# Threshold attention and a maxout layer on one core: the order of the work written out as one list in place of steps

## The chip, the core and the metric

The kernel runs on one core of a Trainium2 chip. Its engines work side by side, each through its own instructions in order: TensorE (PE, with the weight loads as PEld), VectorE (DVE), ScalarE (ACT), GpSimd (POOL), and SyncE (SP), which here only issues DMAs. The metric is the time of one execution on the device in microseconds (us), less is better.

## The reference

Eight batches of eight heads, 576 rows and 64 columns a head. For each head:

```python
scores = scale * q @ k.T                         # 576 x 576
thresh = max(scores, row) - tau                  # tau = 0.02
scores = where(scores >= thresh, scores, -1e9)
attn   = softmax(scores)
x      = attn @ v                                # heads side by side: x is 4608 x 512
```

Then the maxout layer over all 4608 rows, with weights 512 x 768 and 768 x 512:

```python
h   = maximum(maximum(x @ w1, x @ w2), x @ w3)
out = h @ w_out
```

## The kernel before

**Attention.** A quad is four heads of one batch; there are 16 (`quads`), two a batch. `load` and `load_v` (L153, L177) bring a quad in, with ten DMAs on SP. Four pieces a quad (`transposed`, L228: q and k, two pairs of heads each) turn q and k on PE; ScalarE writes the scaled q (`qt`), VectorE writes k (`kt`), GpSimd writes `qs`, a copy of `qt` with the halves of the partitions exchanged (`swapped`, L215). `cast_v` (L193) makes v bf16 on GpSimd. A *chunk* is one block of 128 rows of queries for two of the heads (indices 0 to 8 in a quad, 144 in all). It has two *tiles*, r = 0 and 1, each 128 x 576 scores in float32. For each tile:

- `scores` (L253): matmuls on PE into a PSUM slot, the two halves of the contraction rows at once.
- `maximum` (L280): VectorE finds the row maximum in that slot.
- `exponents` (L291): ScalarE reads the slot and writes `z`. With this the slot is free.
- `numerators` (L299): a tile is *masked* or not (`masked`, L277). If it is, ScalarE has already taken exp, and VectorE zeroes what lies under the threshold and sums (SCALAR_TENSOR_TENSOR). If it isn't, ScalarE has written Prelu with a very flat side, and a second ScalarE pass takes exp and sums.

Then, for the chunk, `normalized` (L308): a reciprocal on VectorE, two products to bf16 on GpSimd (`P`), and a DMA transpose from SP into `pt` ("ptq"). When the nine chunks of a quad are there, `product` (L317) multiplies by v on PE, once for each r, and copies to `xt`, on VectorE or ScalarE or both.

**Maxout layer.** When both quads of a batch are done, `ffn` (L377) yields 18 hidden pieces (6 blocks of 128 columns times w1, w2, w3) and three output pieces. A hidden piece of a whole batch has two halves of eight matmuls, the second behind a wait for the first (`halves`, L355), since both write the same banks. The w1 result goes through ScalarE to `hm`, the others are joined to it by VectorE (`hm`, `hT`). Output pieces go through ScalarE (`ob`, `obr`) and SP to memory. The last batch is done in two parts of 256 and 320 rows.

**PSUM and buffers.** All PSUM is one pool of four slots of 128 x 1024 float32, given out round robin (`slot`, L149). `z` has four buffers, `P` six.

**What sets the order.** `_Ordered` (L53) keeps each of the four compute engines in the order in which the program issues. That order comes from steps, one a chunk (`step`, L573). `others(n)` (L515) chooses what joins step n: what `plan` has for its two half steps (the four transpose pieces of the next quad at half steps 9, 11, 13, 15, the products at PA = 12 and PB = 14 of the quad after), or else a piece each from `todo`, the list of maxout pieces. PE gets these and the scores of chunk n + 1, in an order like this; a and b are halves of pieces, s are scores:

```python
ARRAY = "a0 a1 b0 b1 s0 s1"
ORDER = "V0 A0 R0 K0 V1 M0 M1 A1 N0 K1 N1 E0 E1"
LAG = dict(M=0, E=0, N=1, K=1)
```

ORDER is the same in every step: V and A are the copies out of PSUM on VectorE and ScalarE, M maxima, E exponents, N and K numerators (not masked, masked) of the chunk before, R the normalization. Loads come at the start of a quad's steps (L610 to L613), value casts at step 1 for the first quad and step 3 of each quad for the next, the twelve loads of the weights at steps 12, 14, ... 34 with their casts two steps later. `masked` is the same for all quads: the r = 1 tile of six of the nine chunks, of seven in the first three quads, 99 tiles of 288.

Of the kernel before, what the change touches and what calls it, by code (L numbers as in the profile page):

```python
# [23 lines left out]
EARLY = 3  # L24
MASKED0 = (0, 1, 2, 3, 4, 6, 7)
MASKED = (0, 1, 3, 4, 6, 7)
# [3 lines left out]
ARRAY = "a0 a1 b0 b1 s0 s1"  # L30
ORDER = "V0 A0 R0 K0 V1 M0 M1 A1 N0 K1 N1 E0 E1"
LAG = dict(M=0, E=0, N=1, K=1)
LATE = 0
ED = 40
HOLD = 0
WL = (12, 14, 16, 18, 20, 22, 24, 26, 28, 30, 32, 34)
WC = 2
LQ = 0
LV = 0
NC = 3  # L40
TS = (9, 11, 13, 15)
PA = 12
PB = 14


class _Piece:


    def __init__(self, first, second=None, done=None, on=""):
        self.first, self.second, self.done, self.on, self.needs = first, second, done, on, None  # L50
# [23 lines left out]
def kernel(  # L74
# [23 lines left out]
    tensor, scalar, vector, pool = (_Ordered(tc, e) for e in (nc.tensor, nc.scalar, nc.vector, nc.gpsimd))  # L98
# [18 lines left out]
    def weight_loads():  # L117


        def piece(dst, src):  # L120
            my = {}

            def load():
                my["t"] = stage.tile([128, 4 * 256], F32, name="stage")
                nc.sync.dma_start(out=my["t"].rearrange("p (k f) -> p k f", k=src.shape[1]), in_=src)

            def cast():
                pool.tensor_copy(out=dst, in_=my["t"].rearrange("p (k f) -> p k f", k=src.shape[1]))
            return load, cast
# [11 lines left out]
    zz = ctx.enter_context(tc.tile_pool(name="zz", bufs=4))  # L141
    pp = ctx.enter_context(tc.tile_pool(name="pp", bufs=6))
# [4 lines left out]
    ps_s = ctx.enter_context(tc.tile_pool(name="ps_s", bufs=4, space=PSUM))  # L147

    def slot(name):  # L149
        return ps_s.tile([128, 1024], F32, name=name, tag="s")  # L150


    def load(g, first=False):  # L153
        b, qd = quads[g]
        L = dict(b=b, qd=qd, first=first)
        q2 = nc.scalar if first else nc.sync
# [7 lines left out]
        srcs = (("q", q, nc.sync), ("k", k, q2))  # L164
# [12 lines left out]
    def load_v(g, L):  # L177
# [4 lines left out]
        for h in range(4):  # L182
            nc.sync.dma_start(out=vm[:, h].rearrange("p c d -> p (c d)"),
                              in_=v[b, 4 * qd + h].rearrange("(p c) d -> p (c d)", c=9)[:, 0:512]
                              .rearrange("p (x u) -> p x u", x=2))
        for r in range(2):
            nc.sync.dma_start(out=vr[64 * r:64 * r + 64], in_=src[:, 8, 2 * r:2 * r + 2, :])
# [40 lines left out]
    def transposed(L, n, r):  # L228
# [5 lines left out]
        def first():  # L234
            targets(L, n)
            st["ps"] = ps = slot("tp")
# [7 lines left out]
        def done():  # L244
            off = 320 * r
            evacuated(L, n, r, lambda t: t[:, :, off:off + 64 * nj],
                      st["ps"].rearrange("p (i z) -> p i z", i=2)[:, :, 0:64 * nj])
            if n == "q":
                swapped(L, slice(off, off + 64 * nj))
        return _Piece(first, None, done, "A" if n == "q" else "V")  # L250


    def scores(L, idx, r):  # L253

        ps = slot("sc")
# [21 lines left out]
    def masked(g, idx, r):  # L277
        return r == 1 and idx in (MASKED0 if g < EARLY else MASKED)

# [28 lines left out]
    def normalized(L, idx, z, sm):  # L308
        rs = small.tile([128, 2], F32, name="rs")
        vector.reciprocal(rs, sm)  # L310
        P = pp.tile([128, W], BF16, name="P")
        for n in range(2):
            pool.tensor_scalar(out=P[:, n * S:(n + 1) * S], in0=z[:, n * S:(n + 1) * S],
                                    scalar1=rs[:, n:n + 1], scalar2=1.0, op0=OP.mult, op1=OP.mult)
        nc.sync.dma_start_transpose(out=L["pt"][:, :, idx * 128:(idx + 1) * 128], in_=P)

    def product(L, r, xt, part=None):  # L317
# [11 lines left out]
        def first():  # L329
            st["ps"] = ps = slot("o")  # L330
# [7 lines left out]
        def done():  # L338
            ps = st["ps"]
            dst = xt[:, 2 * L["qd"] + r, :]  # L340
            if part is None and r == 0:
                vector.tensor_copy(out=dst, in_=ps[:, 0:S])
            elif part is None:
                vector.tensor_copy(out=dst[:, 512:S], in_=ps[:, 512:S])
                scalar.activation(out=dst[:, 0:512], in_=ps[:, 0:512], func=AF.Copy)
            elif part == 1:
                scalar.activation(out=dst[:, 0:256], in_=ps[:, 0:256], func=AF.Copy)
            elif r == 0:
                vector.tensor_copy(out=dst[:, 256:S], in_=ps[:, 0:320])
            else:  # L350
                scalar.activation(out=dst[:, 256:S], in_=ps[:, 0:320], func=AF.Copy)
        return _Piece(first, None, done, "A" if part == 1 or part == 2 and r == 1 else "V")
# [24 lines left out]
    def ffn(b, xt, hT, runs, chunks):  # L377


        st = {}  # L380
        nr, n = len(runs), runs[0][1] - runs[0][0]

        def hid(f, wi):
            my = {}

            def start():
                if wi == 0:
                    st["hm"] = hp_.tile([128, nr, n], BF16, name="hm", bufs=3)
                my["hm"], my["ps"] = st["hm"], slot("ph")

            def operands(kc, a):
# [3 lines left out]
                        lambda rows: xt[rows, kc, c0:c1])  # L395

            def first():
                start()
# [8 lines left out]
            def done():  # L407
                hm = my["hm"]
# [3 lines left out]
                else:  # L412
                    dst = hm if wi == 1 else \
                        hT[:, f, runs[0][0]:runs[-1][1]].rearrange("p (a u) -> p a u", a=nr)
                    vector.tensor_tensor(out=dst, in0=pv, in1=hm, op=OP.max)
            return [_Piece(first, (lambda: my["h"][1]()) if nr == 2 else None, done, "V" if wi else "A")]
# [3 lines left out]
        def outp(c):  # L420
# [3 lines left out]
            def first():  # L424
                my["ps"] = ps = slot("po")
                my["h"] = halves([[(ps[:, 512 * a:512 * a + 512],
                                    lambda rows, a=a, f=f: hT[rows, f, (c + a) * 128:(c + a) * 128 + 128],
# [3 lines left out]
            def done():  # L431
                for a in range(2):
                    ob = hp_.tile([128, DM], F32, name="ob", bufs=4)
                    scalar.activation(out=ob, in_=my["ps"][:, 512 * a:512 * a + 512], func=AF.Copy)
                    nc.sync.dma_start(out=rows_out[:, (0, 2, 1, 3)[c + a]:8:4], in_=ob)
            return [_Piece(first), _Piece(lambda: my["h"][1](), None, done, "A")]

        def ninth():
# [3 lines left out]
            def first():  # L442
                my["ps"] = ps = slot("po")
                for f in range(NF):
                    for x in range(2):
                        tensor.matmul(ps[64 * x:64 * x + 64, :256], hT[:, f, 512:S], wo[:, f, 256 * x:256 * x + 256],
                                      start=(f == 0), stop=(f == NF - 1))

            def done():
                ob = hp_.tile([128, DM // 2], F32, name="obr", bufs=2)  # L450
                scalar.activation(out=ob, in_=my["ps"][:, :256], func=AF.Copy)
                for x in range(2):
                    nc.sync.dma_start(out=rows_out[:, 8, 256 * x:256 * x + 256], in_=ob[64 * x:64 * x + 64])
            return [_Piece(first, None, done, "A")]

        return ([pc for f in range(NF) for wi in range(3) for pc in hid(f, wi)],
# [12 lines left out]
    Ls, xts, hTs = {}, {}, {}  # L469
    todo, held = [], []  # L470

    def o_step(g, r, part=None):
        b = quads[g][0]
        if b not in xts:
            xts[b] = xp.tile([128, 4, S], BF16, name="xt")
        mine = [product(Ls[g], r, xts[b], part)]
        if r == 1 and quads[g][1] == 1:
            if b not in hTs:
                hTs[b] = hp_.tile([128, NF, S], BF16, name="hT")
            if part is None:  # L480
                runs, chunks = ((0, S // 2), (S // 2, S)), (0, 2, 4)
            elif part == 1:
                runs, chunks = ((0, 256),), (0,)
            else:
                runs, chunks = ((256, S),), (2, 4)
            hids, outs = ffn(b, xts[b], hTs[b], runs, chunks)
            hids[0].needs = mine[0]
            for o in outs:
                o[0].needs = hids[-1]

            todo.extend(hids + held + [p for o in outs[:-1] for p in o])
            held[:] = outs[-1]
        return mine


    plan = {}

    def at(when, fn):
        plan.setdefault(when, []).append(fn)

    prep = [("q", 0), ("k", 0), ("q", 1), ("k", 1)]
    for g in range(NQ - 2):
        for when, a in zip(TS, prep):
            at(18 * g + when, lambda g=g, a=a: [transposed(Ls[g + 1], *a)])
        at(18 * g + 18 + PA, lambda g=g: o_step(g, 0))
        at(18 * g + 18 + PB, lambda g=g: o_step(g, 1))
    e = 18 * y
    for when, a in zip((0, 1, 4, 5), prep):
        at(e + when, lambda a=a: [transposed(Ls[z_], *a)])
    for when, g, pr in zip((15, 17, 23, 25), (y, y, z_, z_), (0, 1, 0, 1)):  # L510
        at(e + when, lambda g=g, pr=pr: o_step(g, pr, 1))
    for when, g, pr in zip((34, 35), (y, y), (0, 1)):
        at(e + when, lambda g=g, pr=pr: o_step(g, pr, 2))

    def others(n):  # L515

        ps = []
        for when in (2 * n, 2 * n + 1):
            if when in plan:
                for fn in plan[when]:  # L520
                    ps.extend(fn())
            else:
                for _ in range(2 if when >= e + ED else 1):
                    if todo and n >= HOLD:
                        ps.append(todo.pop(0))
        return ps

    def issued(ps, scored=()):

        scored = list(scored)
        out = []
        if len(ps) == 2 and ps[0].second and ps[1].needs is not ps[0]:
# [138 lines left out]
```

## Time and profile before

| | |
|---|---|
| three timed runs | 492.9, 493.21, 494.25 us (median 493.21) |
| profiled execution | span 493.0 us, first to last instruction |
| TensorE's mean granted clock | 0.965 |
| VectorE: row maxima | 288 of about 750 ns |
| VectorE: second pass of masked tiles | 99, mean 886 ns |
| ScalarE: exponents, second pass, its accumulator read | 288 of 741, 189 of 692, 189 of 210 ns |
| GpSimd: normalization | 288 of 768 ns, two a chunk |
| GpSimd: `qs` copies; value casts; weight casts | 62 of 835; 16 of 1134 and 32 of 290; 12 of about 1100 ns |
| DMA transposes | 144, each 1.3 us of SP's issue, landing after 3.8 us (3.2 to 7.6) |

Rows of the profile name an engine, an operation and "out<-in" by the names of the tiles: `sc` scores, `nm` and `unused` the maxima (masked or not), `z` exponents, `rs` reciprocals, `P` and `ptq` the normalized block and its transpose, `o` products with v, `tp` transposes, `ph` hidden, `po` outputs. A wait "A <- B" says that A sat idle until B ended. All compute lines carry L62, the helper in `_Ordered`, so rows are told apart by tiles.

### The profile page before, as it was taken

To read this page: it belongs to the slowest core of one execution; us is meant where nothing else is said; L and a number is where in the kernel's file an instruction comes from. 1 tells how busy PE (TensorE), PEld (TensorE's weight loads), DVE (VectorE), ACT (ScalarE), POOL (GpSimd) and SP (SyncE) were. 2 spreads that over 40 slices of the span, in tenths; PEclk is the share of its full clock that TensorE was granted. 3 is DMA by queue.
4 is the path that set the end of the run, shared out by engine and by line. 5 is a ranking of instruction groups with operands and counts; after the bars stand their busy time and mean duration, and the time that the engine had idled before them with its cause. 6 is when DMAs were issued, how large, how long until landed. Compare 5 with 4: busy or idle time off the path is not lost.

```text
span 493.0 us, 14020 instructions
## 1 busy us (share of the span) xinstructions
PE 457.5 (93%) x5188; PEld 309.4 (63%) x5188; DVE 401.2 (81%) x996; ACT 394.5 (80%) x814; POOL 308.4 (63%) x416
## 2 busy tenths in 40 slices
PE   7777879979999999999999999999999989999995
PEld 5434437747477675767577675867567665676672
DVE  3998977968799979899798978899799998788350
ACT  3998978857998889888998889889898897886322
POOL 3797989876675757475665857475665776444000
PEclk8797978979999999999999999999999999999999
DMA  7899999999999999969699879979696556854402
GB/s 222 278 195 224 183 263 206 252 237 229 187 210 192 191 196 207 213 138 202 141 231 169 175 158 203 217 132 201 148 238 145 99 96 147 143 100 93 126 12 97
DMA packets 213285, 87.44 MB, mean 177 GB/s; under 512 B 186336, under 2 KB 200160, under 8 KB 213216
## 3 DMA queue, kind: packets, MB, share of 16 engines
q1 hardware_dynamic: 212656, 85.95, 83.3%
q8 instruction: 41, 0.67, 0.6%
q10 hardware_dynamic: 560, 0.59, 0.4%
q14 instruction: 28, 0.23, 0.2%
HBM read 34.60 MB, written 9.44 MB: 89 GB/s over the span
## 4 chain that ended last, share of the span: by engine, by line
PE 54%; DVE 12%; POOL 11%; ACT 11%; issue 7%; DMA 5%; SPq 0%; ACTq 0%; POOLq 0%; DVEq 0%
PE ph L62 21%; PE sc L62 18%; PE po L62 8%; ACT z L62 8%; POOL P L62 7%; PE o L62 5%; DVE unused L62 5%; DMA ptq<-P 3%; DVE z L62 3%; POOL qs L62 2%; DVE nm L62 2%; PE tp L62 1%; ACT ob L62 1%; DVE hm L62 1%; DMA qm<-in_q_dram 1%
## 5 line engine op out<-in xcount | busy, mean ns | idle before, releaser
L62 POOL TENSOR_SCALAR P<-z,rs 128x576 bf16<-128x576 f32 x288 | 217.5, 768 | 121.7 <-DVE rs L62 95.7
L62 ACT ACTIVATE z<-sc,nm 128x576 f32<-128x576 f32 x288 | 198.1, 741 | 51.3 <-DVE unused L62 28.5
L62 PE MATMUL sc<-kt,qs 64*128 64x256 f32 (+2 forms) x640 | 193.4, 444 | 11.6 <-ACT z L62 9.8
L62 PE MATMUL sc<-kt,qt 64*128 64x320 f32 (+2 forms) x640 | 194.3, 456 | 7.3 <-ACT z L62 7.0
L62 DVE TENSOR_SCALAR_CACHE_REDUCE unused<-sc 128x576 bf16<-128x576 f32 x189 | 138.4, 749 | 30.9 <-PE sc L62 30.4
L62 PE MATMUL ph<-xt,w 64*128 64x288 bf16 (+2 forms) x2160 | 162.1, 283 | 1.2 <-ACT z L62 0.6
L62 PEld LDWEIGHTS <-w 64*128 64x128 bf16 (+1 forms) x2160 | 127.4, 94 | 31.8 <-issue 11.8
L62 ACT ACTIVATE z<-z 128x576 f32<-128x576 f32 x189 | 129.5, 692 | 0.0
L62 PEld LDWEIGHTS sc<-kt,qs 64*128 64x128 f32 (+1 forms) x640 | 92.3, 184 | 44.0 <-ACT z L62 34.0
L62 PEld LDWEIGHTS sc<-kt,qt 64*128 64x128 f32 (+1 forms) x640 | 92.8, 184 | 29.5 <-ACT z L62 27.0
L62 DVE SCALAR_TENSOR_TENSOR z<-z 128x576 f32<-128x576 f32 x99 | 87.7, 886 | 0.0
L62 DVE TENSOR_REDUCE nm<-sc 128x1 f32<-128x576 f32 x99 | 74.5, 752 | 1.1 <-PE sc L62 1.0
L62 POOL COPY qs<-qt 64x640 f32<-64x640 f32 (+1 forms) x62 | 51.8, 835 | 14.7 <-ACT qt L62 11.7
L62 DVE TENSOR_TENSOR hm<-ph,hm 128x576 bf16<-128x576 f32 (+2 forms) x54 | 37.3, 690 | 23.9 <-PE ph L62 14.3
L62 PE MATMUL po<-wo,hT 64*128 64x512 bf16 (+1 forms) x480 | 52.4, 357 | 0.4
L62 PE MATMUL o<-ptq,vb 128*64 128x64 bf16 (+2 forms) x544 | 42.3, 293 | 4.0 <-DMA ptq<-P 4.0
L62 PEld LDWEIGHTS <-hT 64*128 64x128 bf16 (+1 forms) x480 | 26.2, 97 | 23.8 <-issue 5.1
L62 ACT ACTIVATE hm<-ph 128x576 bf16<-128x576 f32 (+2 forms) x54 | 32.2, 597 | 11.1 <-PE ph L62 11.1
L62 PEld LDWEIGHTS <-vb 128*64 128x64 bf16 x544 | 23.1, 114 | 26.8 <-issue 14.8
L62 ACT ACTIVATION_READ_ACCUMULATOR z<-z 128x1 f32 x189 | 39.7, 210 | 0.0
L62 DVE TENSOR_TENSOR hT<-ph,hm 128x576 bf16<-128x576 f32 (+2 forms) x54 | 37.1, 687 | 2.5 <-PE ph L62 0.8
L62 ACT ACTIVATE qt<-tp 128x640 f32<-128x640 f32 (+1 forms) x32 | 21.1, 660 | 9.3 <-PE tp L62 9.3
(30 smaller groups left out, 246.7 us busy)
## 6 DMA issues: line engine op xcount, KB each, us to landing
vm<-in_v_dram SPq DMA_DIRECT2D x64, 128.0 KB, 2.9
out_dram<-ob SPq DMA_DIRECT2D x32, 256.0 KB, 2.6
qm<-in_q_dram SPq DMA_DIRECT2D x15, 512.0 KB, 4.5
km<-in_k_dram SPq DMA_DIRECT2D x15, 512.0 KB, 5.3
stage<-in_moe_w_dram SPq DMA_DIRECT2D x9, 512.0 KB, 4.7
ptq<-P SPq DMA_TRANSPOSE x144, 3.8
stage<-in_moe_w_out_dram SPq DMA_DIRECT2D x3, 512.0 KB, 4.5
qm<-in_q_dram SPq DMA_DIRECT2D x16, 64.0 KB, 3.3
```

Source lines behind the costliest of these rows:

```text
L62: ins = fn(*a, **kw)
```

## The change

The step machinery (`plan`, `others`, `issued`, `step`, `rest` and their constants) goes. In its place stands one string for 2445 pieces of work, read from left to right by `issue`. A letter is one piece of work, taken from the front of a line of work that is ready for that letter. S, T, O and F start scores, transposes, products and maxout pieces on PE and are followed by a digit, the PSUM slot. B is the second half of the oldest maxout piece that has one. Small letters are: m maxima, e exponents, n and k numerators, r reciprocal, p normalization, t the DMA transpose, a and c copies of transposed q and k, q the exchanged copy, h, v and u copies of maxout pieces, w and x copies of products, y value casts, l the loads of a quad, g and z the load and the cast of a piece of weights, o a store.

The four PSUM slots become four pools of one buffer, named by the digit. Which tiles are masked is a string of 288 digits with 106 ones, in either r. SP joins the engines that keep the order of issue. Buffers (`z` 4, `P` 6) and the work on each piece stay as they were.

```diff
-EARLY = 3
-MASKED0 = (0, 1, 2, 3, 4, 6, 7)
-MASKED = (0, 1, 3, 4, 6, 7)
+MASKED = """
+001001010001010101001000111000011001001101001100100100000100100010001000
...
-ARRAY = "a0 a1 b0 b1 s0 s1"
-ORDER = "V0 A0 R0 K0 V1 M0 M1 A1 N0 K1 N1 E0 E1"
...
+ORDER = """
+lS0myeS1nS2mS3emnS0mleS1rpemT2knS3meamT0erqcS2nT1kS0emapS3trmnS1emytemS2ekT0ecpS3lnmS1nS0rmpemnS2kqemeS3meS1
+rkepT0mntS2rampektS0nmT3erctpeS1mnT3S2tkyameS3tnrrmS0pemngS1mpetrkeS2mepS3tmeS0mnS1gqketrnmT2emlpekS3nkO0qem
+nrcS1eprwS2nS3rmnS0pmemeS1mpeO2tmnrkepS3tekS0nmS1ztxwrmepS2rnmtS3ekzetmS0npmS1etmerT2kpntS3marmepS2tkeT0mnS1
+tceermS3pgnT0kgS2emqtaS1rmnO0merepkS3ewS2nmpT1tO0nmecztekS3xzS1wrmngF2pmS0geBkeS3mqhtF1meBrreS2pvS0nmF3nF1mz
...
-    tensor, scalar, vector, pool = (_Ordered(tc, e) for e in (nc.tensor, nc.scalar, nc.vector, nc.gpsimd))
+    tensor, scalar, vector, pool, sync = (
+        _Ordered(tc, e) for e in (nc.tensor, nc.scalar, nc.vector, nc.gpsimd, nc.sync))
...
-    ps_s = ctx.enter_context(tc.tile_pool(name="ps_s", bufs=4, space=PSUM))
-
-    def slot(name):
-        return ps_s.tile([128, 1024], F32, name=name, tag="s")
+    ps_s = ctx.enter_context(tc.tile_pool(name="ps_s", bufs=1, space=PSUM))
+
+    def bank(name, where):
+        return ps_s.tile([128, 1024], F32, name=name, tag=f"s{where}")
...
     def masked(g, idx, r):
-        return r == 1 and idx in (MASKED0 if g < EARLY else MASKED)
+        return by_mask[2 * number[g, idx] + r] == "1"
...
-                    nc.sync.dma_start(out=rows_out[:, (0, 2, 1, 3)[c + a]:8:4], in_=ob)
...
+                stores.append(lambda: sync.dma_start(out=rows_out[:, (0, 2, 1, 3)[c + a]:8:4], in_=ob))
...
+    def issue(what, where):
+        if what == "S":
+            c, r = next(todo["S"])
+            c[r] = scores(Ls[c["g"]], c["idx"], r, where)
+            line["m"].append((c, r))
...
+        elif what == "m":
+            c, r = line["m"].pop(0)
+            c["bias", r] = maximum(c["g"], c["idx"], r, c[r])
+            line["e"].append((c, r))
...
+    while x < len(text):
+        what = text[x]
+        if what in "STOF":
+            x += 1
+        issue(what, int(text[x]) if what in "STOF" else None)
+        x += 1
```

## The prediction

> **What bounds the kernel now.** I read the busy rows and the slices first: an order can only win where the engine that bounds a stage stands still.
>
> ```profile
> PE 457.5 (93%) x5188; PEld 309.4 (63%) x5188; DVE 401.2 (81%) x996; ACT 394.5 (80%) x814; POOL 308.4 (63%) x416
> ...
> PE   7777879979999999999999999999999989999995
> ...
> PEclk8797978979999999999999999999999999999999
> ```
>
> PE is at seven or eight tenths in the first six slices and again in the ninth (98.6 to 111 us), then at nine. So there are stages with different limits. VectorE's timeline gives the borders by the first maximum of a chunk (a chunk is one block of 128 query rows of two heads, two score tiles): chunk 0 at 9.3 us, chunk 18 at 56.2, chunk 26 at 79.7, chunk 36 at 116.1, chunk 126 at 395.2, the last at 449.4. The table of stretches, cut there (length, busy us of PE, PEld, DVE, ACT, POOL, then granted clock, DMA share, GB/s):
>
> ```profile
> 9.30:56.20 46.90, 38.13 (x284) 22.12 (x284) 42.56 (x110) 40.68 (x84) 38.95 (x51) 0.83 0.95 225
> 56.20:79.70 23.50, 18.24 (x142) 10.71 (x141) 18.68 (x50) 18.40 (x39) 20.31 (x25) 0.78 1.11 245
> 79.70:116.10 36.40, 33.33 (x396) 24.17 (x395) 29.27 (x73) 27.77 (x58) 29.79 (x38) 0.91 1.06 232
> 116.10:395.20 279.10, 272.57 (x3296) 187.44 (x3290) 246.50 (x611) 244.05 (x505) 183.21 (x253) 1.00 0.92 183
> ```
>
> To 56.2, DVE (91%) and ACT (87%) set the pace, 2.44 us a chunk where nothing stands. From 56.2 to 79.7 POOL is the fullest (86%) and the DMA share is over 1. From 116.1 on PE is busy 97.7%, at 3.1 us a chunk. The chain of waits inside 95 to 112 us shows what an early stall is made of:
>
> ```profile
> 95.74 0.98 POOL vb L62
> 96.72 0.12 POOL vr L62
> 96.84 7.59 DMA ptq<-P
> 104.43 0.04 issue
> 104.48 2.61 PE o L62 x14
> ```
>
> POOL's value casts delay a softmax block, its transpose goes out late on a full queue, and PE, which runs in order, stands before the product that reads it. Last, the waits of 116.1 to 395.2 (total, times, longest):
>
> ```profile
> PEld sc L62 <- ACT z L62: 30.0, 89, 1.0
> DVE unused L62 <- PE sc L62: 22.5, 39, 2.3
> ...
> PE sc L62 <- ACT z L62: 4.8, 11, 0.5
> ```
>
> Scores wait for a PSUM slot until ScalarE has read what was in it, and DVE then waits for those scores. PE's "busy" hides part of this. In PE's timeline I took the start-to-start time of each group of matmuls between the same neighbours from 125 to 400 us: the sum is 274.1 us, and with each group at its shortest 250.4 (two hidden pieces 1.96 to 2.36, a pair of scores 0.97 to 1.18). So 23.7 us are stalls that an order could at best remove.
>
> **The change, part by part.** The number of matmuls, copies, DMAs and elements stays. I counted the list's letters and set durations from the groups beside them.
>
> *Masked tiles.* 106 in place of 99. A masked tile costs DVE 752 + 886 + 80 against 749 + 82 ns, ACT 741 against 741 + 692 + 210. Seven more: DVE +6.2 us, ACT -6.3. Neither bounds after 116 us (88% and 87% busy), so 0; if DVE were the bound, +6.2. The first 27 chunks hold 21 masked tiles in both. What a masked tile's second pass costs is not steady: 886 ns on the mean, 747 to 1486. The Trainium skill ("SBUF — State Buffer", Who interferes with whom) says that a DVE instruction with two SBUF inputs contends with a GpSimd instruction that reads SBUF. The second pass is such a one, and the spread agrees; by that rule all seven would run at the long end, +4 us more on DVE, hidden as well.
>
> *POOL and loads, chunks 0 to 26 (9.3 to 79.7 us).* The steps did four value casts (steps 1, 3, 12, 21) and seven weight casts (14, 16 up to 26) here, the list does three and four. Out go one value cast (1134 + 2 x 290 = 1.7 us) and three weight casts (3 x 1102 = 3.3): 5.0 us from the engine that is fullest from 56 to 80. The next limit is DVE's pace: chunks 15 to 18 took 10.3 us and 24 to 26 took 8.4, against 7.5 and 5.0 at the undisturbed pace, so at most 6.2 can come back. Against it: the list issues loads at chunks 0, 2.5, 6.5, 14.5 and then 37, the steps at 0, 9, 18, 27, 36. Two loads (1.73 MB each, some 7 to 8 us of DMA at 225 GB/s) move in among the first transposes on SP's queue, and two leave chunks 18 to 36. And the first products come closer to their data: for quad 0 the list has the product 2.5 chunks after the last normalization, for quad 1 three, 6.1 and 7.4 us at 2.44; before, they stood 10.5 and 10.8 us behind it (35.4 to 45.9, 61.0 to 71.8), and still DVE waited for them. Bounds: -6.2 if POOL's relief brings the transposes forward as much, +9 if not (the second rival). I take half of the best, **-3**.
>
> *Chunks 26 to 36 (79.7 to 116.1).* The list still begins the hidden pieces at chunk 25.5, as before. Chunk 33 took 6.8 us against 3.1, the stall of the chain above: 3.7 lost. Two more weight casts land here (+2.2), one value cast leaves (-1.7); the product comes 4.0 chunks after the last normalization, about what it had (11 us). The load that shared the queue at chunks 27 to 30 is gone. Bounds -3.7 to 0; **-3**. A rule that speaks of the same place: "TensorE: Matmul & The Clock Gate" (HAM oscillation) says that a wait over about 3.4 us halves PE's clock. The granted 0.78 to 0.91 against 1.00 later agrees; by the rule each such stall removed gives up to 3.4 us more of full clock.
>
> *Steady part, chunk 36 on (116.1 to 449).* This is the large unknown. In steps, slots went round robin, and a score tile's slot was written again after 2.47 us of other PE work (one score 0.49, four halves 1.97). By my count of the list, with the same prices, the median is 2.46 and the least 1.77; a fifth of the tiles have under 2.12, which is the median time from a score's end to the end of the exponent that frees it (1.64 to 2.76 at the tenth and ninetieth per cent). If that delay stayed as it is, the mean wait would rise from 0.06 to 0.10 us a tile: 45 ns x 180 = +8. But the delay is made of DVE's and ACT's order, which the list rewrites too: it no longer holds both maxima behind the evacuations of the step. If that removes all stalls, -23.7. Between these the middle is -8. Besides, pieces alternate singly (hidden half, score, other half 73 times). A lone score tile has 320 columns on one half of the rows and 256 on the other, 540 against 434 ns, where a pair is even at 485 each: nothing if the streams drift, 54 ns x 150 = +8 if each transition waits. Products that stand next to each other save a switch: a score pair takes 1.36 us ahead of a product and 0.97 ahead of a hidden piece, 0.39 each, five pairs more in the list, -2.0. Bounds -26 to +16; I take **-7**, nearer to nothing than to the best because the room between the uses of a slot has not grown.
>
> *SP's queue and the end.* The DMAs are now held in the list's order. Stores get their own letter, behind their copies, so SP stands less on them (6.9 us on "ob" behind ACT, 15 times); while transposes have 12 us or more between issue and product from 190 us on, that is 0, and at most the 0.9 us of the longest such wait where they have not. After the last score PE runs without gaps in both (449 to 485 before); the list leaves fewer hidden pieces there, work that is only moved. The last copy and store are the same: 0.
>
> Sum, against the profiled span of 493.0 us (the timed runs' median is 493.2, so I set them equal): 493.0 - 3 - 3 - 7 = **480.0 us**.
>
> **The rivals.**
> 1. *The list fits the chip.* All of 6.2 and 3.7 early and three quarters of 23.7 (18): 493 - 28 = 465 us. For it: PE's stalls are short and many (89 and 11), so small shifts could remove them. Against: DVE would be 92% full at 3.0 us a chunk.
> 2. *Slower: early products stand before their transposes.* Before, 8.6 us passed between the normalization of chunk 8 and SP's issue of its transpose (35.4 to 44.0), 6.4 for chunk 17 (61.0 to 67.4), and a landing takes 3.8. The list leaves 6.1 and 7.4 us for 12.4 and 10.2: PE would stand 6.3 and 2.8 us there and hold every score behind it, DVE and ACT with them. Without the early gains and the steady one, 493 + 9 = 502 us. It decides as soon as SP's lag is over 2.3 us at quad 0 and 3.6 at quad 1.
> 3. *New waits for old ones.* Each stall moves to another slot: the early 3 us remain, the steady part gives 0 to -2: 488 to 493, around 490.
>
> **How the numbers follow.** The forecast (470 to 487) has 0.55, the first rival 0.15, the second 0.17, the third 0.13. A difference under 0.3% (1.5 us) cannot be told from none. Faster by over 0.3% (under 491.5): 0.55 + 0.15 + 0.06 of the third = 0.76; within: 0.06; slower: 0.17 and 0.01. The range goes from 465 (first rival) to 497, about half way into the second, whose price also shrinks with what the steady part gives back.
>
> **What would show it.** Early: chunk 26 at about 77 us in place of 79.7, no gap of over 2 us before a product, the ninth slice at eight or nine. Steady: under 3.08 us a chunk, "sc" waiting for "z" for clearly under 35 us between chunks 36 and 126, PE over 97% of the stretch. Masked: 106 second passes, DVE about 407 us in sum, ACT about 388. I am wrong if the products' wait for "ptq" grows past 10 us, if waits for slots stay at 35 us (then the third rival), or if the group times of lone scores are 540 ns.

## The result and the profile after

The changed kernel takes **467.63 us** (median of four runs, 466.39 to 469.02), the kernel before beside it 493.62 (492.9 to 494.25): a ratio of **0.946, 95% interval 0.943 to 0.949**. Its profiled span is 467.2 us against 493.0, so 25.8 us went. I forecast 480.0 and a gain of 13; the range held the time, and the first rival (465) came closer to it than the forecast.

The page of the changed kernel, busy rows and slices:

```profile
PE 439.2 (94%) x5188; PEld 308.6 (66%) x5188; DVE 403.9 (86%) x1003; ACT 395.4 (85%) x800; POOL 328.8 (70%) x416
...
PE   7866889999999999999998999999999999999995
...
PEclk8989999999999999999999899999999999999999
```

PE reaches nine tenths in the seventh slice, has no low slice at 100 us any more, and the clock is at nine tenths or more from the fourth slice on but for one slice. The stretches between the same first maxima as before (chunks 0, 18, 26, 36, 126; columns as before):

```profile
9.40:54.90 45.50, 35.26 (x276) 20.13 (x273) 40.00 (x107) 40.03 (x83) 38.25 (x48) 0.90 1.04 250
54.90:74.70 19.80, 16.47 (x163) 9.43 (x164) 19.74 (x50) 18.29 (x38) 19.34 (x22) 1.00 1.11 205
74.70:103.90 29.20, 28.31 (x364) 19.68 (x361) 27.69 (x71) 26.82 (x57) 26.36 (x32) 1.00 1.15 248
103.90:372.80 268.90, 264.54 (x3305) 190.35 (x3304) 251.20 (x623) 245.58 (x492) 200.36 (x257) 0.99 0.94 195
```

Chunks 0 to 18 are 1.4 us shorter, 18 to 26 3.7, 26 to 36 7.2, and the 90 chunks of the long stretch take 268.9 in place of 279.1 us, 2.99 a chunk. From 54.9 us on DVE is all but full until chunk 26 (busy 19.74 of 19.80). The waits of the whole run, first of the kernel before, then of the changed one (total, times, longest):

```profile
PEld sc L62 <- ACT z L62: 61.0, 139, 3.2
DVE unused L62 <- PE sc L62: 30.4, 50, 2.3
ACT z L62 <- DVE unused L62: 28.5, 62, 1.7
PE sc L62 <- ACT z L62: 16.8, 27, 2.7
```

```profile
PEld sc L85 <- ACT z L85: 25.5, 56, 1.2
ACT z L85 <- DVE unused L85: 12.3, 25, 1.9
DVE unused L85 <- PE sc L85: 9.6, 22, 2.1
...
PE sc L85 <- ACT z L85: 6.8, 16, 0.8
```

The waits in the ring from PE (a slot) to DVE (maximum) to ACT (exponents) and back to PE are what shrank: scores wait 32.3 us for their slots, not 77.8. Between chunks 36 and 126 it is 7.6 + 0.7 us in place of 30.0 + 4.8.

**Where the time went.** Stretches differ in how much PE work falls into them, so I took from each stretch PE's own work, every matmul at its shortest price in the trace of before (399.2 us in all, the same in every kernel). What is left is time that PE lost. The rows from e1 on are the experiments of the next section; "SP held" means that SP keeps the order of the list, "SP free" that it does not:

| lost by PE, us | to chunk 18 | 18–26 | 26–36 | 36–126 | 126–143 | span |
|---|---|---|---|---|---|---|
| before | 30.4 | 12.8 | 8.6 | 32.9 | 5.2 | 493.0 |
| after | 30.1 | 7.1 | 3.7 | 22.1 | 1.0 | 467.2 |
| e1 steps as a list, SP held | 31.4 | 19.1 | 7.8 | 43.8 | 16.7 | 521.7 |
| e2 list to 36, SP held | 30.5 | 7.1 | 4.4 | 49.9 | 15.0 | 509.5 |
| e3 list from 36, SP held | 32.7 | 19.5 | 4.7 | 28.2 | 0.9 | 488.3 |
| e4 list, old masks | 30.3 | 8.2 | 6.1 | 45.6 | 4.9 | 498.2 |
| e5 list, SP free | 34.1 | 7.1 | 5.3 | 21.8 | 0.9 | 472.0 |
| e6 list to 36, SP free | 34.9 | 7.1 | 6.6 | 48.6 | 5.9 | 505.6 |
| e7 list from 36, SP free | 29.1 | 13.0 | 5.9 | 24.6 | 0.9 | 476.4 |
| e8 steps, list's masks | 30.2 | 12.4 | 5.2 | 45.0 | 8.0 | 503.2 |
| e9 list, loads behind | 28.7 | 7.4 | 12.0 | 18.7 | 0.9 | 471.2 |
| e10 list, casts of the steps | 30.2 | 13.0 | 2.8 | 25.8 | 2.3 | 476.9 |
| e11 steps, alternating | 31.9 | 9.7 | 6.4 | 39.8 | 8.5 | 498.6 |
| e12 steps held, list's loads | 30.7 | 9.5 | 8.0 | 40.5 | 6.7 | 498.6 |

The end (3 to 4 us) makes up the rest. Of the 25.8 us, 10.9 came before chunk 36 and 15.0 behind it (10.8 and 4.2). Each row is one execution. Up to chunk 26, before and e11 issue the same work in the same order on every engine (three pieces at the start lie in other slots), and yet e11 loses 9.7 and not 12.8 between chunks 18 and 26; so where SP is free a difference of some 3 us in one early stretch proves nothing by itself. After and e2, the same to chunk 36 and with SP held, differ by at most 0.7.

### The profile page after: what moved, and what is told of

It reads as the page before. It is cut to its first block, busy times and chain, and to the rows that moved or that the text cites. A ratio compares the mean times of both kernels' runs of the same rounds, so it can differ in the third digit from the quotient of the medians.

```text
span 467.2 us, 13933 instructions
## 1 busy us (share of the span) xinstructions
PE 439.2 (94%) x5188; PEld 308.6 (66%) x5188; DVE 403.9 (86%) x1003; ACT 395.4 (85%) x800; POOL 328.8 (70%) x416
## 4 chain that ended last, share of the span: by engine, by line
PE 51%; DVE 15%; POOL 10%; ACT 10%; issue 7%; DMA 5%; SPq 1%; POOLq 0%; ACTq 0%; DVEq 0%
PE ph L85 20%; PE sc L85 18%; ACT z L85 9%; POOL P L85 7%; PE po L85 7%; DVE z L85 6%; PE o L85 5%; DVE unused L85 4%; DMA ptq<-P 3%; DVE nm L85 2%; POOL qs L85 2%; PE tp L85 2%; DVE kt L85 1%; DMA qm<-in_q_dram 1%; SPq L85 1%
## 5 line engine op out<-in xcount | busy, mean ns | idle before, releaser
L85 POOL TENSOR_SCALAR P<-z,rs 128x576 bf16<-128x576 f32 x288 | 238.0, 844 | 96.7 <-DVE rs L85 50.6
L85 ACT ACTIVATE z<-sc,nm 128x576 f32<-128x576 f32 x288 | 206.7, 741 | 34.0 <-DVE unused L85 12.3
L85 PE MATMUL sc<-kt,qs 64*128 64x256 f32 (+2 forms) x640 | 191.1, 427 | 4.9 <-ACT z L85 3.1
L85 PE MATMUL ph<-xt,w 64*128 64x288 bf16 (+2 forms) x2160 | 175.4, 283 | 1.7 <-DVE hm L85 0.4
L85 DVE TENSOR_SCALAR_CACHE_REDUCE unused<-sc 128x576 bf16<-128x576 f32 x182 | 134.4, 749 | 11.0 <-PE sc L85 9.6
L85 ACT ACTIVATE z<-z 128x576 f32<-128x576 f32 x182 | 123.8, 683 | 0.6
L85 DVE SCALAR_TENSOR_TENSOR z<-z 128x576 f32<-128x576 f32 x106 | 94.5, 894 | 2.3 <-ACT z L85 1.8
L85 DVE TENSOR_REDUCE nm<-sc 128x1 f32<-128x576 f32 x106 | 78.3, 747 | 7.1 <-PE sc L85 6.8
L85 POOL COPY qs<-qt 64x640 f32<-64x640 f32 (+1 forms) x62 | 48.0, 774 | 11.1 <-ACT qt L85 7.9
L85 PEld LDWEIGHTS <-vb 128*64 128x64 bf16 x544 | 23.1, 111 | 22.2 <-issue 14.0
L85 ACT ACTIVATION_READ_ACCUMULATOR z<-z 128x1 f32 x182 | 36.2, 199 | 0.0
```

The costliest lines, as they stand in the source:

```text
L85: ins = fn(*a, **kw)
```

## The experiments

All are written in the changed kernel's code as a list, so that the edits are lists, masks and the hold on SP, and in e1, e8, e11 and e12 three lines that bring the last output pieces in the order of before. "Steps" is the order of work that the steps of before made; "SP free" means that the order of SP's DMAs is left to the framework, as in before. Where steps and list are joined (e2, e3, e6, e7), the masks of the list hold for the whole program. My theory at the start was that of the prediction: gains from two places, POOL and loads early, the order of slots later; the rival was that one of the edits I had put at nothing (masks, SP) mattered.

One thing separates four of these runs from before and was not meant to. Before does not give out its slots strictly in turn: in its program the slot of 50 of the 575 pieces was last used three, five, six or seven pieces earlier and not four, about half of these beside output pieces, whose slots come free late. In e1, e8, e11 and e12 the steps name the slots strictly in turn, and PE's scores wait 7.2 to 7.9 us for the copies of output pieces ("PE sc <- ACT ob", ten times); before, e2 and e6 have no such row. Compared with before, these four runs carry that cost too.

**e1, the old steps as a list.** Masks and order of before; SP is held to it.

```diff
-lS0myeS1nS2mS3emnS0mleS1rpemT2knS3meamT0erqcS2nT1kS0emapS3trmnS1emytemS2ekT0ecpS3lnmS1nS0rmpemnS2kqemeS3meS1
+S0S1mmeelS2S3mmnkeeyS0S1rptmmnkeeS2S3rptmmnkeeyS0S1rptmmnkeeT2S3S0aqrptmmnkeeT1S2S3crptmmnneeT0S1S2aqrptmmnk
...
```

> The order of the steps, written as a list: TensorE, VectorE, ScalarE and GpSimd issue exactly what they issued before, in that order, with the masked tiles of before. Only SP's DMAs are new in order: they are held as issued, where before the framework had put the loads of quads 1 and 2 and the first weights ahead of the first transpose. My theory (the gain comes from the order on the other engines): 490 to 494 us, a little early gain from earlier transposes. Rival (holding SP's order gives the early gain of 10.6 us by itself): about 483 us.

Measured: 521.58 us, ratio 1.057 (1.051 to 1.063). Both numbers missed, upward. PE, DVE, ACT and POOL have the instructions of before in the order of before; SP's order and the slots differ. So **SP's order and the slots together cost 27.5 us**. Of this, e12 gives back 20.5 by the places of loads and casts alone, and the waits for `ob` are 7.9. The reason for the larger part is a fact of before that the prediction had overlooked: its SP was not held, and in the trace the framework had brought the loads of quads 1 and 2 and two weight loads ahead of the first transpose. The waits of e1:

```profile
PEld sc L85 <- ACT z L85: 64.8, 137, 5.7
...
ACT z L85 <- POOL P L85: 25.0, 14, 5.4
...
POOL vb L85 <- DMA vm<-in_v_dram: 15.1, 6, 5.3
...
PE tp L85 <- DMA qm<-in_q_dram: 14.9, 6, 7.9
...
PE sc L85 <- ACT ob L85: 7.9, 10, 1.2
```

PE's transposes and POOL's value casts stand before loads that went out too late (before: 2.3 us for the transposes, no such row for the casts), and both engines run in order, so scores and normalizations stand behind them.

**e2 and e3, each half of the list alone, SP held.** e2 is the list up to chunk 36 and the steps after it, e3 the other way round.

```diff
 ...
-1BarS0veS1pmnF3S2meBztmeO0vnpgknF1rezT3rtwBncS2phS0gmnS3mO1eptmekeS2ztS0wxmF3qnmF1eBreByvF2nS0rvnBmplF3hS1ke
+1BarS0veS1pmnF3S2meBztmeO0vnpgknF1rezT3rtwBncS2phS0gmnS3mO1eptmekeS2ztyyqwxrptmneF0BS3S1rptvmmnneelF2F0BBS3S
...
```

> The list up to the scores of chunk 36, then the order of the steps for all that is left, a slot being the one freed first; masked tiles of the list throughout. By the PE time lost in the two traces (span less the matmuls at their shortest) the list gains 10.6 us up to chunk 36 and 15.1 after it. My theory (stages add up): 493.6 - 10.6 = 483 us. Rival (a lead won early is lost again later, because VectorE and ScalarE are the limit there): 488 us or more.

> The order of the steps up to the scores of chunk 36, then the list for all that is left; masked tiles of the list throughout. My theory (stages add up): 493.6 - 15.1 = 478 to 479 us. Rival (the steady gain needs the early lead): 485 us or more.

Measured: e2 511.43 us, 1.036 (1.031 to 1.041); e3 488.87, 0.990 (0.985 to 0.995). Both expectations missed, since they stood on e1 being like before. Against e1 the early half gives 10.2 and the late one 32.7, but these are not prices of the halves, since the masks and the slots differ too. In the table the early half of e2 is that of the list, and the late half of e3 loses 6 us more than the list's: the halves keep most of what they have, but a half in steps with SP held is dear.

**e4, the list with the old masks.** The tiles that are masked are those of before; each numerator keeps its place in the list and changes its engine.

```diff
-001001010001010101001000111000011001001101001100100100000100100010001000
+010101010100010100010101010100010100010101010100010100010100010100010100
...
-lS0myeS1nS2mS3emnS0mleS1rpemT2knS3meamT0erqcS2nT1kS0emapS3trmnS1emytemS2ekT0ecpS3lnmS1nS0rmpemnS2kqemeS3meS1
+lS0myeS1nS2mS3emkS0mleS1rpemT2nkS3meamT0erqcS2nT1kS0emapS3trmnS1emytemS2ekT0ecpS3lnmS1kS0rmpemnS2nqemeS3meS1
...
```

> The list with the masked tiles of before (99, all r = 1), each second pass at the same place in the list but on the engine that the old choice names. My theory (masks only move 6 us between two engines that have slack): 466 to 469 us. Rival (the uneven choice of tiles is what keeps VectorE free when scores end): 472 us or more, with more waiting of scores for ScalarE's exponents.

Measured: 500.25 us, 1.012 (1.008 to 1.017): **32.6 us slower than the list**, on the rival's side. The waits:

```profile
POOL P L85 <- ACT z L85: 48.4, 22, 5.5
...
ACT z L85 <- DVE unused L85: 35.8, 45, 2.5
PEld sc L85 <- ACT z L85: 34.9, 67, 1.7
DVE unused L85 <- PE sc L85: 26.8, 48, 1.6
```

In the list the first of these rows is 7.8. As I read it, a numerator that lands on the other engine at the same place in the list stands at the head of an engine whose next piece was meant to be a maximum or an exponent; what follows there comes late, and the slot with it. That chain is read from the waits and was not tested by itself. With 99 or 106 masked tiles the busy sums hardly differ (DVE 402.7 and 403.9, ACT 399.0 and 395.4). So it is which tile, at which place, that counts here; an order fitted to the old masks was not tried.

**e5, the list with SP free.**

```diff
-    tensor, scalar, vector, pool, sync = (
-        _Ordered(tc, e) for e in (nc.tensor, nc.scalar, nc.vector, nc.gpsimd, nc.sync))
+    tensor, scalar, vector, pool, sync = tuple(
+        _Ordered(tc, e) for e in (nc.tensor, nc.scalar, nc.vector, nc.gpsimd)) + (nc.sync,)
```

> The list, but SP is not held to it: the framework orders the DMAs as it did before the change; the four engines issue exactly as in the list. Theory 1 (with steps, the framework's order of DMAs was worth 27.5 us over the held one, since it puts loads ahead of transposes that still wait; the list places its DMAs so that holding costs nothing): 465 to 470 us, no matter who orders. Theory 2 (the list's own placing of DMAs is a large part of its gain): 478 us or more.

Measured: 473.59 us, 0.956 (0.953 to 0.960), 6.0 slower than the list and between the two theories. By the table all of it lies before chunk 36 (4.0 and 1.6 us); behind it nothing changes. The first product shows where the 4.0 come from:

```profile
48.63 2.05 PE L85 MATMUL o<-ptq,vb 128*64 128x512 bf16 x14 [5.28 <-DMA ptq<-P]
```

GpSimd ends the normalization of chunk 8 at 38.7 us in the list and in e5. With SP free, loads move in ahead of its transpose, which is issued at 44.8 and not at 40.4, and PE stands 5.28 us inside the product.

**e6 and e7, the halves of e2 and e3 with SP free**, so that the half in steps is nearer to before.

> The list up to the scores of chunk 36, then the order of the steps, as in the run before with this cut, but SP not held in either part. If holding SP to the order of the steps is what cost that run its time: 493.6 - 10.6 = 483 us. If the lead itself is lost in the steps' part: 490 us or more.

> The order of the steps up to chunk 36, then the list, SP not held in either part. If the stages add up: 493.6 - 15.1 = 478 to 479 us. If the list from 36 on needs its own DMA order: 485 us or more (held it was 488.9, of which some 7 us were lost before chunk 36 by holding the steps' DMAs).

Measured: e6 506.45 us, 1.023 (1.019 to 1.026); e7 474.47, 0.961 (0.957 to 0.965). **e7 shows that the late gain stands by itself**: from chunk 36 to 143 PE loses 25.5 us against 38.1 in before and 23.1 in the list, with the early part in steps. It even did better than expected. e6 has the list's early part (7.1 and 6.6) and loses more than all of that later, with the list's masks in steps; part of it is the seam, where three chunks took 17.0 us. So e6 does not price the early half.

**e8, the steps with the list's masks, SP free.** A masked r = 0 tile's numerator takes the place K0 in ORDER, ahead of the maxima. The edit is shown against the list of e1:

```diff
-eeT3S0S1crptmmnkeeS2S3rptmmnneelS0S1rptmmnkeeS2S3rptmmnkeeS0S1rptmmnkeeyS2S3rptmmnkeegT0S1S2aqrptmmnkeeT3S0S
+eeT3S0S1crptmmnkeeS2S3rptmmnkeelS0S1rptmmnneeS2S3rptkmmneeS0S1rptmmnneeyS2S3rptkmmkeegT0S1S2aqrptkmmneeT3S0S
...
```

> The order of the steps, SP not held, with nothing changed but which tiles are masked: the list's 106 in place of 99. In the steps all numerators come a chunk late, so no masked pass waits at the head of VectorE for its exponent. My theory (the choice of tiles is worth little by itself; what cost the 32 us with the old tiles in the list is that a second pass stood at a place meant for the other engine): 492 to 498 us. Rival (the uneven choice is itself the gain): 480 us or less.

Measured: 505.15 us, 1.021 (1.017 to 1.024). Neither: 11 us slower than before, worse than the theory and on the other side from the rival. Of the 11, 7.8 are the waits for `ob` that come with the slots; the masks by themselves gain nothing, and what is left of the loss, some 3 us by this estimate, shows in the wait for exponents:

```profile
PEld sc L85 <- ACT z L85: 70.1, 143, 1.7
...
DVE nm L85 <- PE sc L85: 15.4, 17, 2.7
```

This wait for slots, which the list brought from 61.0 to 25.5, is 70.1. **This order does not win without its masks (e4), nor these masks without the order (e8).**

**e9, six loads later in the list** (quads 3, 4 and 11 to 14), each behind the last transpose of the quad whose product is next; only SP differs. It tests the one late stop that the changed kernel has. Its SP from 236 us on (start, time in the queue, DMAs of a kind in a row), then PE:

```profile
240.35 0.40 SPq L85 DMA_DIRECT2D qm<-in_q_dram  x1
...
242.37 2.57 SPq L85 DMA_DIRECT2D vm<-in_v_dram  x4
244.98 1.29 SPq L85 DMA_DIRECT2D vr<-in_v_dram  x2
246.37 11.10 SPq L85 DMA_TRANSPOSE ptq<-P  x7
```

```profile
253.44 0.38 PE L85 MATMUL o<-ptq,vb 128*64 128x512 bf16 x1
255.76 1.12 PE L85 MATMUL o<-ptq,vb 128*64 128x512 bf16 x14 [1.94 <-DMA ptq<-P]
...
258.02 0.74 PE L85 MATMUL sc<-kt,qs 64*128 64x320 f32 x1
```

The ten loads of a quad hold SP's queue for 6 us, the transposes go out behind them, and the product of quad 8 stops PE for 1.94 us.

```diff
-T0cS1eBlrmF0npS3veBmF2yhrS1keBmnF0pS3veBmnF2vntS1rurS0pemS2tF3mepmetS1keS0mnBtmerkS2epoT1umF0uokatrS3nkqT1eB
+T0cS1eBrmF0npS3veBmF2yhrS1keBmnF0pS3veBmnF2vntS1rurS0pemS2tF3mepmetlS1keS0mnBtmerkS2epoT1umF0uokatrS3nkqT1eB
...
```

> The list, with six of the fifteen loads of a quad (for quads 3, 4, 11, 12, 13, 14) moved behind the last transpose of the quad whose product comes next; nothing but SP's order differs. In the list's trace SP issues a load from 240.4 to 246.3 us, six transposes queue behind it, and the product of quad 8 stands from 253.4 to 255.8, the clock halved after it; the stretch of chunks 72 to 90 loses 7.2 us of PE time where its neighbours lose 3.2 to 3.8. Theory (products stand on transposes that queue behind loads on SP): that stretch falls to under 5 us lost, 462 to 466 us in all. Rival (the product waits for GpSimd's late normalization, or the loads then come too late): 467 us or more.

Measured: 472.09 us, 0.956 (0.953 to 0.958), 4.5 slower than the list, where I expected a gain. The stop is gone as expected: chunks 72 to 90 lose 4.0 in place of 7.2, and chunks 0 to 18 also lose less (28.7 for 30.1). But chunks 26 to 36 lose 12.0 in place of 3.7. The chain of e9 shows why:

```profile
70.48 5.39 DMA stage<-in_moe_w_dram
...
77.25 1.04 POOL w L85
78.29 1.44 POOL P L85 x2
...
80.44 0.62 POOL qs L85
...
81.10 1.43 PE sc L85 x3
```

The ten loads of quad 4 now stand on SP's queue from 62.89 us, ahead of a pair of weight loads, which left at 70.48 and not at 66.10. POOL then stood 6.4 us before the weight cast, and the exchanged q (`qs`) behind it held the scores for 5.5. It is the same theory with another victim. Only the last four loads moved would by the table be worth some 3 us (an estimate, 7.2 less 4.0); that was not tried.

**e10, the list with the casts of the steps.** The letters y, g and z stand where the steps had them; everything else is the list.

```diff
-lS0myeS1nS2mS3emnS0mleS1rpemT2knS3meamT0erqcS2nT1kS0emapS3trmnS1emytemS2ekT0ecpS3lnmS1nS0rmpemnS2kqemeS3meS1
+lS0meS1nS2mS3yemnS0mleS1rpemT2knS3meamT0erqcS2ynT1kS0emapS3trmnS1emtemS2ekT0ecpS3lnmS1nS0rmpemnS2kqemeS3meS1
...
```

> The list, with value casts, weight loads and weight casts at the places that the steps gave them (three weight casts and one value cast more by chunk 26); the rest of the list as it is. My prediction's early term (5.0 us of GpSimd work out of the stretch where GpSimd is fullest): 470 to 473 us, the loss before chunk 26 up by 3 to 5 us. Rival (GpSimd's relief is worth nothing, the early gain is the order of the rest): 467 to 469 us.

Measured: 480.86 us, 0.974 (0.970 to 0.978), 13.2 slower than the list and more than expected. Its profiled span was 476.9, so the table shows 9.7 of that: chunks 18 to 26 lose 13.0 as in before (12.8), where the list loses 7.1. Behind chunk 36 it loses 5.0 more than the list, which no theory of mine had. Most of the early loss is one stop, in a product of quad 1:

```profile
71.60 2.07 PE L85 MATMUL o<-ptq,vb 128*64 128x512 bf16 x14 [5.00 <-DMA ptq<-P]
```

**The early gain is undone by these places, but GpSimd's load is not what does it here.** GpSimd ends the normalization of chunk 17 at 62.7 us in e10 and at 62.6 in the list. But SP issues four weight loads between its transposes from 50 to 66.6 us, where the list has none from 43.5 to 66.1, and the transpose of chunk 17 goes out at 66.7 and not at 63.3 and lands at 71.55 and not at 66.7. The casts and the weight loads moved together, so no run prices GpSimd's relief by itself. The gain of chunks 26 to 36 is not undone (2.8 lost).

**e11, steps with pieces in alternation.** Old masks, SP free; in steps with two halved hidden pieces PE alternates halves and scores, and the evacuations, maxima and exponents alternate with them. Put as the constants of the steps, for those steps alone:

```diff
-ARRAY = "a0 a1 b0 b1 s0 s1"
-ORDER = "V0 A0 R0 K0 V1 M0 M1 A1 N0 K1 N1 E0 E1"
+ARRAY = "a0 s0 b0 a1 s1 b1"
+ORDER = "R0 M0 N0 V0 A0 K0 E0 M1 V1 N1 A1 K1 E1"
```

> The steps, SP not held, masked tiles of before; where a step has two halved pieces TensorE alternates (half, score, half; half, score, half) in place of four halves and two scores, and VectorE and ScalarE follow that order (maximum, copy, exponent; maximum, copy, exponent). Theory (the steady gain is the alternation, which frees VectorE for a maximum as soon as its score ends): 480 to 487 us, waits of scores for exponents well under the 35 us of before. Rival (it needs the fitting of every piece): 491 us or more.

Measured: 502.88 us, 1.017 (1.014 to 1.021), the rival's side. Of the 9.6 us over before, 7.2 are the waits for `ob` that come with the slots, so the alternation costs little by itself, but it is no gain. The median time from a score's end to its maximum fell to 0.15 us, like the list's 0.18, but the ninetieth per cent stayed at 1.05 (list 0.58), and slots are still waited for 68.8 us in sum (before 77.8):

```profile
PEld sc L85 <- ACT z L85: 51.4, 97, 2.1
...
PE sc L85 <- ACT z L85: 17.4, 34, 1.6
```

**e12, e1 with the list's loads and casts.** The old steps and masks, SP held, but l, y, g and z at the list's places; shown against e1:

```diff
-S0S1mmeelS2S3mmnkeeyS0S1rptmmnkeeS2S3rptmmnkeeyS0S1rptmmnkeeT2S3S0aqrptmmnkeeT1S2S3crptmmnneeT0S1S2aqrptmmnk
+lS0yS1mmeeS2S3mmnkeeS0lS1rptmmnkeeS2S3rptmmnkeeS0S1rptmmnkeeT2S3yS0aqrptmmnkeeT1S2lS3crptmmnneeT0S1S2aqrptmm
...
```

> The steps written as a list with SP held (521.6 us), but loads of quads, value casts, weight loads and weight casts at the list's places. If the 27.5 us that holding cost come from loads and casts placed for an order that was not held: 500 us or less. If they come from the stores and transposes themselves standing in the order of issue: 512 us or more.

Measured: 501.10 us, 1.015 (1.012 to 1.017). It gives back 20.5 of the 27.5 us of e1, close to the bound that the theory gave. PE's transposes wait 1.9 us for `qm` in place of 14.9, and the row of `vb` is gone. So the places of the loads and casts made a held SP dear. The 7.8 us that remain over before are about the 7.9 that scores wait for `ob` here, so with the list's places the hold itself seems to cost next to nothing.

## Why the prediction was right in its direction and half in its size

**Masked tiles, 0: right in the sum, wrong as a reason.** 106 second passes came, DVE was busy 403.9 us (407 forecast), ACT 395.4 (388 forecast). ACT's second passes and their reads fell by 9.2 us of busy time (169.2 to 160.0), but the exponents, with the same count and mean, went from 198.1 to 206.7: in the records they overlap their neighbours less, so the busy sum did not fall. The words "Neither bounds" took the engines as sums. They run in order: a numerator moved to the other engine shifts what is behind it, and with the old masks the list is 32.6 us slower (e4). That the 0 held in the sum is luck: this list works only with its own masks.

**POOL and loads, chunks 0 to 26, −3: the bound was right, the cause was not shown.** The bound was 6.2, measured 0.3 + 5.7 = 6.0; I took half for the sake of the second rival, which had two places. PE did stop inside two products, at quad 0 for 1.71 us (the profile names no releaser, but the transpose of chunk 8 lands at 44.98 us and PE goes on at 45.1) and later at quad 8 for 1.94 behind "ptq", and never as long as the 6.3 us that I priced. The term paid for 5.0 us less work on GpSimd. With the casts and weight loads put back, 5.9 us of loss come back (e10), but by way of SP's queue.

**The second rival had its condition right.** It was to decide as soon as SP's lag, from a normalization to the issue of its transpose, was over 2.3 us at quad 0 or 3.6 at quad 1. In the changed kernel the lags are 1.8 and 0.7 us, and PE stands 1.71 and 0.33. In e5 the lag is 6.2 us at quad 0 and PE stands 5.28; in e10 it is 4.0 at quad 1 and PE stands 5.00. What kept this rival away is the order on SP.

**The loads' places: a wrong premise.** I wrote that the steps load at chunks 0, 9, 18, 27. In the trace of before they stood earlier, since SP was not held. It did not spoil the sum, since the list happens to place its loads well; that is luck. But the step that put SP's queue at 0 failed: the places of loads and casts on a held SP are worth 20.5 us in steps (e12 against e1), and holding SP is worth 6.0 in the list (e5). "Slots went round robin", in the prediction and ahead of it, is not quite so either, as the waits for `ob` above show.

**Chunks 26 to 36, −3: near, 4.9 measured.** No product stands there any more, and chunk 33 takes 4.8 us in place of 6.8. The cause is not isolated: in steps the loss is also only 4.7 to 5.9 with the list's masks (e3, e7, e8) and 6.4 in e11. The rule on TensorE's clock that I weighed here (the Trainium skill, "TensorE: Matmul & The Clock Gate", HAM oscillation) has its row: granted 1.00 in both stretches from 54.9 to 103.9 us, where it was 0.78 and 0.91. It also has a row against it: behind the stop of 1.94 us at quad 8, well under 3.4, the granted clock is 0.65 from 256 to 260 us, and matmuls that take 0.43 and 0.38 us took 0.74 and 0.63.

**Steady part, −7: the term that was mis-sized; it measured −15.0.** I put the value near the low end because "the room between the uses of a slot has not grown". By its count that is true, and it was the wrong measure. What changed is the other side: tile by tile from the traces, chunks 36 to 126, from the end of a score to its maximum 0.18 in place of 0.34 us on the median, 0.58 in place of 1.09 at the ninetieth per cent, to the end of the exponent 1.92 in place of 2.12. The sum of the stalls (23.7) covered 125 to 400 us, about chunks 39 to 127; there the list took 10.8 of it, somewhat under half. The other 4.2 came behind chunk 126, which the sum did not cover. The two costs I set against it were small. The waits for slots, +8 if the delay stayed, fell from 34.8 to 8.3 us. A lone score between two hidden halves, where no wait lies in it (61 times), takes 495 ns on the mean against 485 in a pair, so some 0.6 us (61 x 10 ns) and not 8. Single ones do take 540: in a run of them they come as about 431 and 539 ns in turn, and two cost what a pair does, so the streams drift. DVE is 93% full at 2.99 us a chunk, and this did not stop the gain.

**What is shown of the steady part, and what is open.** Shown: it stands without the early part (e7); it is neither the masks alone (e8) nor an alternation of the kind of e11 alone; without its own masks the order loses it (e4). Open: which piece of the order of DVE and ACT gives most, and what the list's choice of slots gives; slots named strictly in turn cost 7 to 8 us in steps, so the choice is not free. The sum of the parts is far from the whole: no part tried alone in steps gains (e1, e8, e11), and each one undone in the list costs 6 to 33 us (e4, e5, e10).

**The rivals.** The first nearly came true in both its parts (10.9 early for 9.9, 15.0 later for 18). The third (new waits for old ones) did not: the waits went down by more than half. "PE over 97%" and "under 3.08 us a chunk" came as written (98.4%, 2.99), chunk 26 came at 74.7 and not 77.

## What to carry to other kernels

Where several engines run in order and hand slots round a ring, price an edit by what stands behind each moved piece on its engine, not by the engine's busy sum: a fitted order gains as a whole, and one part of it taken out can cost more than the whole gains (e4 lost 32.6 us, the change had gained 26). Before you reason on when a load is issued, read its time on the DMA queue in the trace; the program's text does not say it unless that queue is held. If stalls are many and short and the same work has a shortest time in the trace, their sum over a stretch is a fair bound for that stretch, and here a fitted list took somewhat under half of it. When an old order is written anew as a control, compare its waits for slots with the original's before you call one difference the only one.

## What I had not expected of the hardware

GpSimd's normalization became slower with the shorter span, 844 in place of 768 ns, and DVE's second pass a little (894 for 886). The group of the changed kernel (busy us, mean ns, idle before):

```profile
L85 POOL TENSOR_SCALAR P<-z,rs 128x576 bf16<-128x576 f32 x288 | 238.0, 844 | 96.7 <-DVE rs L85 50.6
```

That is 20.5 us more on GpSimd with no more work, and I see no wait that it made longer, POOL being busy 75% of the long stretch. With the list's masks in steps it is 826 (e8), in steps with the old masks and SP held 780 (e1). The rule of the Trainium skill weighed in the prediction ("SBUF — State Buffer", Who interferes with whom) would go this way, but no run here isolates it. The second thing is the granted clock, which fell behind a stop of 1.94 us: 1.00 from 250 to 256 us, 0.65 from 256 to 260. The stretch of chunks 72 to 90 lost 3.2 us more with that stop than without it (e9), so the slow matmuls cost about 1.3 beyond the wait, an estimate from one execution of each.
